# First product of six experts by Strassen's seven half-size products in a mixture-of-experts kernel

## The chip, the cores and the metric

One NeuronCore of a Trainium2 chip runs the whole program. The metric is device time in microseconds (us), the median of several executions of the same program; lower is better. TensorE is called PE here, its weight loads PEld, VectorE is DVE, ScalarE is ACT, GpSimd is POOL, SyncE is SP.

## The reference

Attention with a recurrent state gives one row of 320 numbers for each of 3072 tokens; a balanced gate gives each token a weight for each of 8 experts; every expert works on every token. The part that matters here is the experts:

```
N, D, E, F = (3072, 320, 8, 1024)
for e in range(E):
    h = np.maximum(x @ w1[e], 0.0)
    ye = h @ w2[e]
    out += P[:, e:e + 1] * ye
```

The gate `P` comes from 8 rounds of dividing by the row sums and then by the column sums ("P /= P.sum(1) + 1e-09", then "P /= P.sum(0) + 1e-09", then "P *= N / E").

## The kernel before

The attention runs first, in 24 units of 128 tokens, and expert 0 runs between its stages. Then come experts 1 to 7. The order of all work is a hand-written plan: `at(slot, fn)` puts a function into a numbered slot, and the slots are emitted in order of their number, so that every engine gets its instructions in this order and works through them strictly in turn. Engines wait for each other by semaphores.

Numbers in the experts are float32, multiplied as sums of a high and a low part (`w1h`, `w1l`, `hh`, `hl`). The activations x lie transposed in `xt`, 128 partitions by five rows of 3072 tokens: rows 0 and 1 are the high parts of the first 256 of the 320 dimensions, rows 2 and 3 their low parts, row 4 holds the high and the low part of the last 64 dimensions, one above the other.

A step of an expert is one block of 128 hidden units with 512 tokens (256 tokens in expert 0, and in the last two blocks of expert 7):

- `p1` (L103), the first product: 8 matmuls of 512 columns into one PSUM bank `ph`. Six are high*high, high*low and low*high for two halves of 128 dimensions; two are for the last 64 dimensions.
- `relu` (L112, L113): ACT makes `hh` from `ph`, then DVE makes `hl`.
- `p2` (L125), the second product: 12 matmuls of 320 columns (4 tiles of 128 tokens, 3 pairs of parts), with a slice of `hh` or `hl` as weights, summed over the 8 hidden blocks of the expert in four PSUM banks `py`.
- after the eighth hidden block `evac` (L137) adds `py` times the gate into `acc` on DVE, four tiles at a time.

`p1` runs two steps ahead of `p2`. Tokens are the outer loop, hidden blocks the inner one. The weights of the next expert are loaded by SP and split by POOL (L78 to L81) while an expert runs; expert 1's are split by ACT and POOL while expert 0 ends. The rounds of the gate (`sinkhorn`) stand in the plan at the change from expert 0 to expert 1, one stage each 1.25 slots: a stage `rows` is five DVE instructions on `logits` (L746 to L750), a stage `columns` is one small matmul pair on PE (`pc`, L753) and three DVE instructions (L755 to L757). The first such matmul follows `pb` (L740).

Of the kernel before, what the change touches and what calls it, by code (L numbers as in the profile page):

```python
# [16 lines left out]
def f32(ap):  # L17
    return ap.bitcast(F32)
# [3 lines left out]
def mlstm_moe_kernel(ctx, tc, q, k, v, i_gate, f_gate, o_gate, moe_w_gate, moe_w1, moe_w2, out):  # L22
# [16 lines left out]
    wa = ctx.enter_context(tc.tile_pool(name="wa", bufs=KF))  # L39
# [13 lines left out]
    wts = {}  # L53

    raws = {}

    def load_raw(pool, e, f):
        w1r = pool.tile([128, 3, 128], F32, tag="w1r", name="w1r")
        w2r = pool.tile([128, DM], F32, tag="w2r", name="w2r")
        cols = slice(f * 128, (f + 1) * 128)  # L60
        nc.sync.dma_start(w1r[:, 0:2, :], moe_w1[e, 0:256, cols].rearrange("(k p) f -> p k f", p=128))
        nc.sync.dma_start(w1r[0:DR, 2, :], moe_w1[e, 256:DM, cols])
        nc.sync.dma_start(w1r[DR:128, 2, :], moe_w1[e, 256:DM, cols])
        nc.sync.dma_start(w2r, moe_w2[e, cols, :])
        raws[e, f] = (w1r, w2r)

    def split_w(pool, e, f):
        """hi/lo parts of expert e's f-th 128 hidden columns."""
        w1r, w2r = raws.pop((e, f))
        w1h = pool.tile([128, 3, 128], F32R, tag="w1h", name="w1h")  # L70
        w1l = pool.tile([128, 3, 128], F32R, tag="w1l", name="w1l")
        w2h = pool.tile([128, DM], F32R, tag="w2h", name="w2h")
        w2l = pool.tile([128, DM], F32R, tag="w2l", name="w2l")
        if e == 1:
            nc.scalar.copy(w1h, w1r)
            nc.scalar.copy(w2h, w2r)
        else:
            nc.gpsimd.tensor_scalar(w1h, w1r, 1.0, 1.0, op0=ALU.mult, op1=ALU.mult)  # L78
            nc.gpsimd.tensor_scalar(w2h, w2r, 1.0, 1.0, op0=ALU.mult, op1=ALU.mult)
        nc.gpsimd.tensor_sub(w1l, w1r, f32(w1h))  # L80
        nc.gpsimd.tensor_sub(w2l, w2r, f32(w2h))  # L81
        wts[e, f] = (w1h, w1l, w2h, w2l)

# [1 line left out]
    class Moe:  # L85
        """Steps (expert, first tile, tiles, hidden blocks); the first product runs ahead of the second."""

        def __init__(self, hp, ps_h, ps_y):
            self.hp, self.ps_h, self.ps_y = hp, ps_h, ps_y
            self.h = {}  # L90
            self.y = {}

# [13 lines left out]
        def relu(self, e, t0, n, fs):  # L106
            nf = len(fs)
            ph = self.h[e, t0, fs]
            hh = self.hp.tile([128, nf, n * 128], F32R, tag="hh", name="hh")
            hl = self.hp.tile([128, nf, n * 128], F32R, tag="hl", name="hl")  # L110
            flat = lambda x: x.rearrange("p a t -> p (a t)")
            nc.scalar.activation(flat(hh), flat(ph), AF.Relu)  # L112
            nc.vector.scalar_tensor_tensor(flat(hl), flat(ph), 0.0, f32(flat(hh)), op0=ALU.max, op1=ALU.subtract)  # L113
            self.h[e, t0, fs] = (hh, hl)

        def p2(self, e, t0, n, fs):
            hh, hl = self.h.pop((e, t0, fs))
            if fs[0] == 0:
                self.y[e, t0] = [self.ps_y[j // 2].tile([128, 512], F32, tag="py", name="py") for j in range(n)]
            ys = self.y[e, t0]  # L120
            for a, f in enumerate(fs):
                _, _, w2h, w2l = wts[e, f]
                for w, h, first, last in ((w2h, hh, True, False), (w2l, hh, False, False), (w2h, hl, False, True)):
                    for j in range(n):
                        nc.tensor.matmul(ys[j][:, 0:DM], h[:, a, j * 128:(j + 1) * 128], w,  # L125
                                         start=f == 0 and first, stop=f == KF - 1 and last)
            if fs[-1] == KF - 1:
                self.evac(e, t0, n, self.y.pop((e, t0)))

        def evac(self, e, t0, n, ys):  # L130
            for j in range(n):
                t = t0 + j
                a, y = acc[:, t, :], ys[j][:, 0:DM]
                if e == 0:
                    nc.scalar.copy(a, y)
                    continue
                nc.vector.scalar_tensor_tensor(a, y, logits[:, t, e:e + 1], a, op0=ALU.mult, op1=ALU.add)  # L137
                if e == E - 1:
                    r = TILE_ROW[t]
                    nc.sync.dma_start(out[r * 128:(r + 1) * 128, :], a)  # L140

# [6 lines left out]
    def attention_phase():  # L148
        es = ExitStack()
        hp = ctx.enter_context(tc.tile_pool(name="hp", bufs=3))  # L150
# [9 lines left out]
        # (their scratch lies where the last tokens' sums come to lie)  # L160
# [26 lines left out]
        def gates_scan():  # L187
            """The running maximum, and the decay summed from each chunk's start."""
# [9 lines left out]
            # rows 0: the state's factor, 32: the key's factor in the next state, 64: the key's log weight  # L198
# [5 lines left out]
        def gates_rows():  # L204
            """The factors by token, and the states' over whole chunks."""
# [16 lines left out]
        def gate_weights():  # L222
            """The experts' gate weights: columns hi | lo."""
# [21 lines left out]
        def first_split(f, a):  # L245
            if a == 0:
                w1r = raw1[:, :, f * 128:(f + 1) * 128]
                w1h = wa.tile([128, 3, 128], F32R, tag="w1h", name="w1h")
                w1l = wa.tile([128, 3, 128], F32R, tag="w1l", name="w1l")
                nc.vector.tensor_copy(w1h, w1r)  # L250
                nc.gpsimd.tensor_sub(w1l, w1r, f32(w1h))
                wts[0, f] = (w1h, w1l) + wts[0, f]
            else:
                w2r = raw2[:, f, :]
                w2h = wa.tile([128, DM], F32R, tag="w2h", name="w2h")
                w2l = wa.tile([128, DM], F32R, tag="w2l", name="w2l")
                nc.vector.tensor_copy(w2h, w2r)
                nc.vector.tensor_sub(w2l, w2r, f32(w2h))
                wts[0, f] = (w2h, w2l)
# [32 lines left out]
        class Unit:  # L292
            """One chunk of one batch: its stages, each a method, in the order in which they run."""
# [23 lines left out]
            def split_hi(self, key):  # L317
                """First parts: q as (1, 2, 3) and (1, 1, 2), k as (3, 2, 1) and (2, 1, 1)."""
# [131 lines left out]
            def split_state(self, x):  # L450
                """The state's parts, as (3, 2, 1, 1)."""
# [53 lines left out]
        def gate(t0, n):  # L505
# [3 lines left out]
            # x's parts times both halves of the columns  # L509
# [281 lines left out]
```

## Time and profile before

| what | value |
|---|---|
| median of 3 runs | 1583.11 us (1582.42 to 1583.76) |
| span of the profiled execution, first to last instruction | 1580.5 us; its own device time is not listed, the median of the runs is 2.6 us above its span |
| PE busy | 1522.0 us, 96% of the span, 9719 matmuls |
| PEld busy | 1397.6 us, 88% |
| DVE busy | 633.3 us, 40% |
| ACT busy | 465.7 us, 29% |
| POOL busy | 378.7 us, 24% |
| mean granted clock of PE | 0.997 of full speed |

Busy time is the sum of the durations of an engine's instructions, and the share is of the span. A matmul row of the timeline gives the start of a group of like matmuls, the time from the first one's start to the last one's end, and their number; since matmuls are pipelined, the spacing of two starts is what one costs, and its duration is when its result is there. A bracket behind a row is the engine's idle time before it and what ended it.

### The profile page before, as it was taken

How to read it: one execution, taken by the hardware profiler on the slowest of the kernel's cores; microseconds unless marked ns; L12 is line 12 of the kernel's file. 1: busy time of each engine (PE TensorE's matmuls, PEld its weight loads, DVE VectorE, ACT ScalarE, POOL GpSimd, SP SyncE). 2: the span in 40 equal slices, each digit the busy share in tenths (PEclk: the TensorE clock that was granted, in tenths of full speed). 3: DMA queues.
4: the chain of work that ended last, by engine and by line, in shares of the span. 5: the costliest groups of instructions: out<-in, count | busy, mean ns of one | idle time of the engine just before them, and what ended most of it. 6: DMA issues, size and time to landing. Idle time of an engine off the chain costs nothing.

```text
span 1580.5 us, 24047 instructions
## 1 busy us (share of the span) xinstructions
PE 1522.0 (96%) x9719; PEld 1397.6 (88%) x9719; DVE 633.3 (40%) x1228; ACT 465.7 (29%) x976; POOL 378.7 (24%) x511
## 2 busy tenths in 40 slices
PE   3699999999999999999999999999999999999999
PEld 2699998998999999999999999999999999999998
DVE  5998898867222222222222222222222222222222
ACT  5677777733222211111111111111111111111111
POOL 5876676628100500031001400050003200000000
PEclk9999999999999999999999999999999999999999
DMA  9999999924000200011000200020001000000000
GB/s 207 210 193 197 198 176 186 190 56 130 27 1 1 74 1 1 0 44 30 1 0 8 67 1 1 1 70 5 0 1 34 13 1 1 1 0 17 34 18 34
DMA packets 271503, 88.12 MB, mean 56 GB/s; under 512 B 205440, under 2 KB 270784, under 8 KB 271392
## 3 DMA queue, kind: packets, MB, share of 16 engines
q1 hardware_dynamic: 271248, 86.29, 26.8%
q8 instruction: 76, 1.25, 0.3%
q10 hardware_dynamic: 144, 0.30, 0.1%
q14 instruction: 35, 0.29, 0.1%
HBM read 55.21 MB, written 6.18 MB: 39 GB/s over the span
## 4 chain that ended last, share of the span: by engine, by line
PE 84%; POOL 4%; DVE 4%; issue 3%; DMA 2%; ACT 2%; SPq 0%; DVEq 0%; POOLq 0%; ACTq 0%
PE ph L103 42%; PE py L125 39%; DMA kn<-in_k_dram 1%; DMA qs<-qp 1%; POOL pl L368 1%; POOL w L314 1%; PE pss L353 1%; POOL rk L327 1%; PE pyy L385 1%; POOL qn L327 0%; DVE den L480 0%; PE pyy L387 0%; DVE acc L484 0%; POOL qp L335 0%; POOL vv L375 0%
## 5 line engine op out<-in xcount | busy, mean ns | idle before, releaser
L113 DVE SCALAR_TENSOR_TENSOR hl<-ph,hh 128x512 fp32r<-128x512 f32 (+1 forms) x440 | 273.2, 621 | 890.1 <-ACT hh L112 889.9
L103 PE MATMUL ph<-xt,w1h 128*128 128x512 f32 (+1 forms) x2200 | 592.0, 366 | 0.9 <-DVE hl L113 0.9
L112 ACT ACTIVATE hh<-ph 128x512 fp32r<-128x512 f32 (+1 forms) x440 | 238.8, 543 | 1026.6 <-PE ph L103 1025.3
L103 PEld LDWEIGHTS ph<-xt,w1h 128*128 128x128 f32 x2200 | 380.0, 189 | 45.2 <-DVE hl L113 1.2
L103 PE MATMUL ph<-xt,w1l 128*128 128x512 f32 (+1 forms) x1320 | 403.5, 363 | 0.0
L125 PE MATMUL py<-w2h,hh 128*128 128x320 f32 x1536 | 300.6, 311 | 0.0
L125 PE MATMUL py<-w2h,hl 128*128 128x320 f32 x1536 | 296.8, 309 | 0.0
L125 PE MATMUL py<-w2l,hh 128*128 128x320 f32 x1536 | 296.8, 309 | 0.0
L103 PEld LDWEIGHTS ph<-xt,w1l 128*128 128x128 f32 x1320 | 241.8, 189 | 40.8
L125 PEld LDWEIGHTS py<-w2h,hh 128*128 128x128 f32 x1536 | 252.2, 189 | 26.6
L125 PEld LDWEIGHTS py<-w2l,hh 128*128 128x128 f32 x1536 | 243.6, 188 | 0.0
L125 PEld LDWEIGHTS py<-w2h,hl 128*128 128x128 f32 x1536 | 243.5, 188 | 0.0
L78 POOL TENSOR_SCALAR w1h<-w1r 128x384 fp32r<-128x384 f32 x48 | 24.9, 518 | 653.9 <-PE ph L103 653.9
L137 DVE SCALAR_TENSOR_TENSOR acc<-py,logits,acc 128x320 f32<-128x320 f32 x168 | 81.0, 544 | 2.1 <-PE py L125 2.1
L368 POOL TENSOR_TENSOR pl<-w,ph 128x512 fp32r<-128x512 f32 x48 | 63.1, 1314 | 57.2 <-ACT ph L367 57.1
L310 ACT ACTIVATE w<-w,gr 128x128 f32<-128x128 f32 x192 | 65.8, 393 | 1.5 <-DMA w<-gd 1.5
L80 POOL TENSOR_TENSOR w1l<-w1r,w1h 128x384 fp32r<-128x384 f32 x56 | 56.9, 1016 | 25.9 <-DMA w1r<-in_moe_w_dram 20.7
L353 PE MATMUL pss<-qs,ks 120*128 120x128 bf16 x384 | 33.2, 238 | 28.5 <-DMA ks<-kp 17.6
L387 PE MATMUL pyy<-vv,pl 128*128 128x42 f32 x192 | 53.2, 280 | 5.7 <-POOL pl L368 5.7
L385 PE MATMUL pyy<-vv,ph 128*128 128x84 f32 x192 | 54.1, 286 | 3.9 <-ACT ph L367 3.0
L353 PEld LDWEIGHTS <-ks 120*128 120x128 bf16 x384 | 25.3, 107 | 30.5 <-DMA ks<-kp 17.6
L81 POOL TENSOR_TENSOR w2l<-w2r,w2h 128x320 fp32r<-128x320 f32 x56 | 49.5, 884 | 0.0
(121 smaller groups left out, 930.2 us busy)
## 6 DMA issues: line engine op xcount, KB each, us to landing
w<-gd SPq DMA_DIRECT2D x24, 512.0 KB, 6.2
w2r<-in_moe_w_dram SPq DMA_DIRECT2D x56, 160.0 KB, 2.4
w1r<-in_moe_w_dram SPq DMA_DIRECT2D x56, 128.0 KB, 2.2
qn<-in_q_dram SPq DMA_DIRECT2D x24, 160.0 KB, 3.5
kn<-in_k_dram SPq DMA_DIRECT2D x24, 160.0 KB, 3.0
vn<-in_v_dram SPq DMA_DIRECT2D x24, 160.0 KB, 3.5
acc<-in_o_gate_dram SPq DMA_DIRECT2D x24, 160.0 KB, 3.2
out_dram<-acc SPq DMA_DIRECT2D x24, 160.0 KB, 1.8
```

The source lines that it names most:

```text
L80: nc.gpsimd.tensor_sub(w1l, w1r, f32(w1h))
L81: nc.gpsimd.tensor_sub(w2l, w2r, f32(w2h))
L103: nc.tensor.matmul(ph[:, a, :], w[:, kw, :], xt[:, kx, cols], start=i == 0, stop=i == len(seq) - 1)
L112: nc.scalar.activation(flat(hh), flat(ph), AF.Relu)
L113: nc.vector.scalar_tensor_tensor(flat(hl), flat(ph), 0.0, f32(flat(hh)), op0=ALU.max, op1=ALU.subtract)
L125: nc.tensor.matmul(ys[j][:, 0:DM], h[:, a, j * 128:(j + 1) * 128], w, start=f == 0 and first, stop=f == KF - 1 and last)
L137: nc.vector.scalar_tensor_tensor(a, y, logits[:, t, e:e + 1], a, op0=ALU.mult, op1=ALU.add)
L310: nc.scalar.activation(w[:, h, :], w[:, h, :], AF.Exp, bias=bias)
L353: nc.tensor.matmul(ps[:, j * L:(j + 1) * L], self.t["k"][0:3 * D, i, :], self.t["q"][0:3 * D, i, :], start=w == 0, stop=w == 1)
L368: nc.gpsimd.tensor_sub(flat(pl), p, f32(flat(ph)))
L385: nc.tensor.matmul(py[:, yo:yo + 2 * V2], ph[:, j, :], self.vv[:, h].rearrange("p a d -> p (a d)"), start=True, stop=False, skip_group_che ...
L387: nc.tensor.matmul(py[:, yo:yo + V2], pl[:, j, :], self.vv[:, h, 0, :], start=False, stop=True, skip_group_check=True)
```

## The change

Experts 2 to 7 take their first product in another way; the attention, expert 0's arithmetic and all second products keep theirs.

The unit of work is now (expert `e`, pair of hidden blocks `g`, pair of token blocks `p`): 256 hidden units and 1024 tokens, four of the old steps; there are 6*4*3 = 72. `g` is the outer loop, `p` the inner one. The first 256 dimensions, the 256 hidden units and the 1024 tokens are cut in half each, and the eight half-size products become seven by Strassen's scheme (Winograd's form). Each product is 3 matmuls of 512 columns (`product`), the last 64 dimensions are added by 4*2 matmuls (`rest`). Four PSUM banks A, B, C, D take the products, DVE adds them up with the sums `u2`, `u3`, `c22` in SBUF (L259), and ACT, DVE and POOL make the four pairs `hh`, `hl` (L266 to L271). The two halves of the second product are 24 matmuls each (`second`): half 0 at the end of the unit, half 1 in the middle of the next unit. Its banks are summed into `acc` after each pair of hidden blocks, 8 tiles a unit, not after eight blocks.

The sums of x that Strassen needs are made once (`combine`, POOL and ACT, while expert 1 runs), those of the weights once for each (e, g) (`w_sums` on POOL, `w_split` on ACT and POOL, 24 times). Expert 1 goes through all tokens twice, with hidden blocks 0 to 3 and then 4 to 7; weights and `hh`, `hl` share one tile `wz`; and the stages of the gate stand (x1 + 10.9 - o) / 19 = 0.93 slots apart, where they were 1.25 apart.

The core of the diff (allocation, loads and placing of weights are left out):

```diff
+        def w_sums(self, e, g):
+            st = late["st"].rearrange("p (a f) -> p a f", f=128)
+            for o, x, y in ((T1, W12, W11), (T3, W22, W12), (WRD, WR1, WR2), (T2, W22, T1), (T4, W21, T2)):
+                nc.gpsimd.tensor_sub(st[:, o, :], st[:, x, :], st[:, y, :])
...
+            nc.scalar.copy(w[:, 0:n], r)
+            nc.gpsimd.tensor_sub(w[:, n:2 * n], r, f32(w[:, 0:n]))
...
+            for i, (s, m) in enumerate(((0, hi), (0, lo), (1, hi))):
+                nc.tensor.matmul(ps, w1[:, s, w - 1, :], m, start=start and i == 0, stop=i == 2, skip_group_check=True)
...
+            for s in range(2):
+                nc.tensor.matmul(ps, w1[:, s, w - 1, :], xt[:, 4, col], start=False, stop=s == 1, skip_group_check=True)
...
+            for a in blocks:
+                h = self.HS[half * 2 + a]()
+                hh, hl = h[:, 0:512], h[:, 512:1024]
+                seq += [(w2[:, 0, a, :], hh), (w2[:, 1, a, :], hh), (w2[:, 0, a, :], hl)]
+            order = [(i, j) for i in range(6) for j in range(4)]
+            if tiles_outer:
+                order = [(i, j) for j in range(4) for i in range(6)]
+            for i, j in order:
+                w, h = seq[i]
...
+            mul = lambda slot, n, x, w, start=True: do(slot, lambda: self.product(bank(n), e, g, p, x, w, start))
+            rem = lambda slot, n, half, w: do(slot, lambda: self.rest(d[n], e, g, p, half, w))
+            add = lambda slot, o, x, n: do(slot, lambda: nc.vector.tensor_add(tp(o), d[n], tp(x)))
+            def h_parts(slot, half, a, n=None, x=None, clamp=False):
+                h = self.HS[half * 2 + a]()
+                hh, hl = h[:, 0:512], h[:, 512:1024]
+                src = lambda: d[n] if n else tp(x)
+                if clamp:
+                    do(slot, lambda: nc.scalar.activation(tp(x), tp(x), AF.Relu))
+                    do(slot, lambda: nc.scalar.copy(hh, tp(x)))
+                    do(slot, lambda: nc.gpsimd.tensor_sub(hl, tp(x), f32(hh)))
+                else:
+                    do(slot, lambda: nc.scalar.activation(hh, src(), AF.Relu))
+                    do(slot + 0.05, lambda: nc.vector.scalar_tensor_tensor(hl, src(), 0.0, f32(hh), op0=ALU.max, op1=ALU.subtract))
+            mul(0, A, (0, 0), W11)
+            do(0.5, lambda: nc.scalar.copy(tp(u2), d[A]))
+            mul(1, B, S2, T2)
+            add(1.5, u2, u2, B)
+            mul(2, C, S3, T3)
+            rem(2, C, 1, WR2)
+            add(2.5, u3, u2, C)
+            mul(3, D, S1, T1)
+            add(3.5, c22, u3, D)
+            mul(5, D, S4, W22, False)
+            rem(5, D, 0, WR2)
+            add(5.5, u2, u2, D)
+            h_parts(5.6, 0, 1, x=u2)
+            mul(6, C, (1, 1), T4)
+            rem(6, C, 1, WRD)
+            add(6.5, u3, u3, C)
+            mul(7, A, (1, 0), W21, False)
+            rem(7, A, 0, WR1)
+            h_parts(7.5, 0, 0, n=A)
+            h_parts(7.7, 1, 1, x=c22, clamp=True)
+            h_parts(7.8, 1, 0, x=u3, clamp=True)
+            def half(i):
+                ys = [self.ps_y[j // 2].tile([128, 512], F32, tag="py", name="py") for j in range(4)]
+                self.second(e, g, p, i, ys, (1, 0), i == 1)
+                for j in range(4):
+                    evac(e, (2 * p + i) * 4 + j, ys[j], e == E - 1 and g == NG - 1)
+            do(8, lambda: half(0))
+            return out_, lambda: half(1)
...
+        whole(t[0], 0, 1)
+        whole(t[1], 1, 1)
+        nc.gpsimd.tensor_add(t[2], t[0], t[1])
+        whole(t[3], 0, 0)
+        nc.gpsimd.tensor_sub(t[4], t[3], t[0])
+        nc.gpsimd.tensor_sub(t[5], t[2], t[3])
+        split(S1, t[2])
+        whole(t[0], 1, 0)
+        split(S3, t[4])
+        nc.gpsimd.tensor_sub(t[1], t[0], t[5])
+        split(S2, t[5])
+        split(S4, t[1])
...
-        for fn in sinkhorn(late):
+        stages = sinkhorn(late)
+        step = (x1 + 10.9 - o) / len(stages)
+        for fn in stages:
             at(o, fn)
-            o += LATE["sinkhorn_step"]
+            o += step
...
+        def prep(x, e, g):
+            at(x, fast.w_load, e, g)
+            at(x + 3.1, fast.w_sums, e, g)
+            at(x + 4.1, fast.w_split, e, g, 0)
+            at(x + 4.2, fast.w_split, e, g, 1)
+        todo = [(e, g) for e in range(2, E) for g in range(NG)]
+        prep(x - 12, *todo[0])
+        for i, (e, g) in enumerate(todo):
+            for p in range(3):
+                if p == 1 and i + 1 < len(todo):
+                    prep(x + 0.9, *todo[i + 1])
+                items, rest = fast.unit(e, g, p)
+                for slot, fn in items:
+                    at(x + slot, fn)
+                at(x + 4, tail.pop())
+                tail.append(rest)
+                x += 9
```

What order the engines get shows at three places. First PE inside the experts, before: the rows of one step (`ph` is the first product, `py` the second).

```order
L103 MATMUL ph<-xt,w1h 128x512 x4
L103 MATMUL ph<-xt,w1l 128x512 x2
L103 MATMUL ph<-xt,w1h 128x512
L103 MATMUL ph<-xt,w1l 128x512
L125 MATMUL py<-w2h,hh 128x320 x4
L125 MATMUL py<-w2l,hh 128x320 x4
L125 MATMUL py<-w2h,hl 128x320 x4
```

PE inside the experts, now: one unit from its first product on (psA to psD are the banks; L218 is `product`, L224 is `rest`; the `py` row in the middle is half 1 of the unit before).

```order
L218 MATMUL psA<-xt,wz 128x512 x3
L218 MATMUL psB<-xs,wz 128x512 x3
L218 MATMUL psC<-xs,wz 128x512 x3
L224 MATMUL psC<-xt,wz 128x512 x2
L218 MATMUL psD<-xs,wz 128x512 x3
L239 MATMUL py<-wz 128x320 x24
L218 MATMUL psD<-xs,wz 128x512 x3
L224 MATMUL psD<-xt,wz 128x512 x2
L218 MATMUL psC<-xt,wz 128x512 x3
L224 MATMUL psC<-xt,wz 128x512 x2
L218 MATMUL psA<-xt,wz 128x512 x3
L224 MATMUL psA<-xt,wz 128x512 x2
```

The row after these is half 0, 24 more `py` matmuls, and then the next unit's psA. Where four steps had 32 matmuls of 512 columns and 48 of 320, a unit has 29 and 48.

Second DVE in the same unit, now (before, it had eight `hl` of L113 and then four sums of L137 for each block of 512 tokens):

```order
L259 TENSOR_TENSOR tp<-psB,tp 128x512
L259 TENSOR_TENSOR tp<-psC,tp 128x512
L259 TENSOR_TENSOR tp<-psD,tp 128x512
L158 SCALAR_TENSOR_TENSOR acc<-py,logits,acc 128x320 x4
L259 TENSOR_TENSOR tp<-psD,tp 128x512
L271 SCALAR_TENSOR_TENSOR wz<-tp,wz 128x512
L259 TENSOR_TENSOR tp<-psC,tp 128x512
L271 SCALAR_TENSOR_TENSOR wz<-psA,wz 128x512
L158 SCALAR_TENSOR_TENSOR acc<-py,logits,acc 128x320 x4
```

`tp` holds u2, u3 and c22, and `wz` here the pairs `hh`, `hl`. Five additions of a bank are new, and a tile is summed into `acc` four times for each expert instead of once.

Third PE at the change from expert 0 to expert 1, between matmuls of the gate (`pc`), before:

```order
L753 MATMUL pc<-cs,onesf 128x8
L125 MATMUL py<-w2h,hh 128x320 x2
L125 MATMUL py<-w2l,hh 128x320 x2
L125 MATMUL py<-w2h,hl 128x320 x2
L103 MATMUL ph<-xt,w1h 128x512 x4
L103 MATMUL ph<-xt,w1l 128x512 x2
L103 MATMUL ph<-xt,w1h 128x512
L103 MATMUL ph<-xt,w1l 128x512
L125 MATMUL py<-w2h,hh 128x320 x2
L125 MATMUL py<-w2l,hh 128x320 x2
L125 MATMUL py<-w2h,hl 128x320 x2
L753 MATMUL pc<-cs,onesf 128x8
```

And now, at the same steps of expert 1:

```order
L964 MATMUL pc<-cs,onesf 128x8
L146 MATMUL py<-wz,h_72 128x320 x6
L116 MATMUL ph<-xt,xs 128x512 x8
L964 MATMUL pc<-cs,onesf 128x8
L146 MATMUL py<-xs,wz 128x320 x12
L116 MATMUL ph<-xt,xs 128x512 x8
L964 MATMUL pc<-cs,onesf 128x8
```

One first and one second product lie between two `pc` now, where three products lay between them at this place before. All eight `pc` now come before the sixth step of expert 1; before, three of them came after it.

## Rows read from the trace of the kernel before

**Rows 1.** The page, part 1: busy time, share of the span, instructions

```profile
PE 1522.0 (96%) x9719; PEld 1397.6 (88%) x9719; DVE 633.3 (40%) x1228; ACT 465.7 (29%) x976; POOL 378.7 (24%) x511
```

**Rows 2.** The page, part 4: the chain that ended last, by engine

```profile
PE 84%; POOL 4%; DVE 4%; issue 3%; DMA 2%; ACT 2%; SPq 0%; DVEq 0%; POOLq 0%; ACTq 0%
```

**Rows 3.** Windows: stretch; PE, PEld, DVE, ACT, POOL busy; clock; DMA

```profile
150.00:200.00 50.00, 46.84 (x434) 45.36 (x434) 41.58 (x97) 37.36 (x94) 34.18 (x47) 0.97 1.05 190
...
700.00:800.00 100.00, 100.00 (x559) 90.72 (x558) 25.13 (x40) 16.77 (x28) 15.29 (x22) 1.00 0.09 24
1000.00:1100.00 100.00, 100.00 (x558) 90.59 (x557) 26.99 (x44) 16.24 (x28) 22.01 (x32) 1.00 0.10 30
```

**Rows 4.** Timeline of one step: start, us, engine, line, count, [idle]

```profile
1000.88 1.09 PE L103 MATMUL ph<-xt,w1h 128*128 128x512 f32 x4
...
1002.49 0.39 PE L103 MATMUL ph<-xt,w1l 128*128 128x512 f32 x1
...
1002.71 0.74 PE L125 MATMUL py<-w2h,hh 128*128 128x320 f32 x4
1002.91 0.60 ACT L112 ACTIVATE hh<-ph 128x512 fp32r<-128x512 f32 x1 [2.99 <-PE ph L103]
...
1003.54 0.69 DVE L113 SCALAR_TENSOR_TENSOR hl<-ph,hh 128x512 fp32r<-128x512 f32 x1 [2.90 <-ACT hh L112]
...
1004.47 0.39 PE L103 MATMUL ph<-xt,w1h 128*128 128x512 f32 x1
```

**Rows 5.** Groups by form: busy us, mean ns, idle before

```profile
L137 DVE SCALAR_TENSOR_TENSOR acc<-py,logits,acc 128x320 f32<-128x320 f32 x168 | 81.0, 544 | 2.1 <-PE py L125 2.1
...
L368 POOL TENSOR_TENSOR pl<-w,ph 128x512 fp32r<-128x512 f32 x48 | 63.1, 1314 | 57.2 <-ACT ph L367 57.1
...
L81 POOL TENSOR_TENSOR w2l<-w2r,w2h 128x320 fp32r<-128x320 f32 x56 | 49.5, 884 | 0.0
...
L359 DVE TENSOR_TENSOR w<-pss,w 128x512 f32<-128x512 f32 x48 | 32.5, 677 | 2.0 <-POOL w L314 1.9
...
L534 ACT ACTIVATE acc<-acc 128x1280 f32<-128x1280 f32 x5 | 6.4, 1274 | 0.1
...
L534 ACT ACTIVATE acc<-acc 128x640 f32<-128x640 f32 x2 | 1.5, 736 | 0.0
```

**Rows 6.** Timeline of PE, 150 to 200 us

```profile
190.20 0.64 PE L103 MATMUL ph<-xt,w1h 128*128 128x256 f32 x4
...
191.15 0.46 PE L125 MATMUL py<-w2h,hh 128*128 128x320 f32 x2
...
195.12 0.61 PE L353 MATMUL pss<-qs,ks 120*128 120x128 bf16 x8 [2.12 <-DVE xt L501]
```

**Rows 7.** One line's durations: ns min/median/max, first and last start

```profile
L749 DVE TENSOR_TENSOR logits<-logits,rs x8: 358/643/1210, 361.2 to 392.1; 128x192 f32<-128x192 f32 x8
```

**Rows 8.** Timeline of PE at the gate's rounds, 358 to 402 us

```profile
358.93 0.38 PE L740 MATMUL pb<-m,onesf 1*128 1x1 f32 x2
...
362.20 0.39 PE L753 MATMUL pc<-cs,onesf 128*128 128x8 f32 x2
...
363.40 1.09 PE L103 MATMUL ph<-xt,w1h 128*128 128x512 f32 x4
...
366.02 0.39 PE L753 MATMUL pc<-cs,onesf 128*128 128x8 f32 x2 [0.62 <-DVE cs L750]
...
370.17 0.39 PE L753 MATMUL pc<-cs,onesf 128*128 128x8 f32 x2
...
374.09 0.28 PE L753 MATMUL pc<-cs,onesf 128*128 128x8 f32 x2
...
381.73 1.09 PE L103 MATMUL ph<-xt,w1h 128*128 128x512 f32 x4
...
400.79 1.09 PE L103 MATMUL ph<-xt,w1h 128*128 128x512 f32 x4
```

**Rows 9.** Windows of PE: stretch; PE busy; granted clock; DMA

```profile
193.00:194.00 1.00, 0.00 (x1) 1.00 1.28 290
...
197.00:198.00 1.00, 1.00 (x9) 0.50 1.06 303
```

More of the change, by code (lines that the diff above doesn't have):

```diff
@@ L67, in split_w @@
[L67 to L76, printed above, removed]
[L77 to L79 removed]
+    W1S, W2S = 2 * 768, 2 * DM
@@ L117, in p2 @@
             hh, hl = self.h.pop((e, t0, fs))
-            if fs[0] == 0:
+            (f,) = fs
+            first, last = (f == 0, f == KF - 1) if e == 0 else (f % 4 == 0, f % 4 == 3)
+            if first:
                 self.y[e, t0] = [self.ps_y[j // 2].tile([128, 512], F32, tag="py", name="py") for j in range(n)]
             ys = self.y[e, t0]
[L121 to L140, printed above, removed]
+            _, _, w2h, w2l = wts[e, f]
@@ new lines, in p2 @@
+            seq = [(w2h, hh), (w2l, hh), (w2h, hl)]
+            order = [(i, j) for i in range(3) for j in range(n)]
+            if last and e:
+                order = [(i, j) for j in range(n) for i in range(3)]
+            for i, j in order:
+                w, h = seq[i]
+                nc.tensor.matmul(ys[j][:, 0:DM], h[:, 0, j * 128:(j + 1) * 128], w,
+                                 start=first and i == 0, stop=last and i == 2)
+            if last:
+                ys = self.y.pop((e, t0))
+                for j in range(n):
+                    evac(e, t0 + j, ys[j], False)
@@ new lines, in combine, with whole, split @@
+    def combine(p, q):
+        S1, S2, S3, S4 = range(4)
+        tp = late["tp"].rearrange("p a t -> p (a t)")
+        t = [tp[:, a * 256:(a + 1) * 256] for a in range(6)]
+        col = [slice((2 * p + half) * 512 + q * 256, (2 * p + half) * 512 + (q + 1) * 256) for half in range(2)]
+        to = slice(q * 256, (q + 1) * 256)
+        xs = late["xs"]
+        def whole(o, k, half):
+            nc.gpsimd.tensor_add(o, f32(xt[:, k, col[half]]), f32(xt[:, k + 2, col[half]]))
+        def split(i, x):
+            hi, lo = xs[:, p, i, 0, to], xs[:, p, i, 1, to]
+            nc.scalar.copy(hi, x)
+            nc.gpsimd.tensor_sub(lo, x, f32(hi))
+        whole(t[0], 0, 1)
[10 more added lines that the diff above has]
+        split(S4, t[1])
@@ L694, in attention_phase @@
[L694 to L703 removed]
+            at(max(o, x1 + 2 + 8 * (t // 4) + 2 * (t % 4)), weigh_first, t)
@@ L704, in attention_phase @@
+        for a in range(2):
+            at(x1 + 16 + 14 * a, combine, 0, a)
+            at(x1 + 54 + 11 * a, combine, 1, a)
+            at(x1 + 76 + 10 * a, combine, 2, a)
+        x = x0
+        tail = []
         for i in range(len(steps) + look):
```

183 lines of the change are left out of this document (131 added, 52 removed).

## The prediction

> **What bounds the kernel now.** I read the page from the whole to the part. Part 1 gives PE 96% of the span and 9719 matmuls [rows 1]; the reader should take from it only that PE is the candidate, since a busy share is an average. Part 4, the chain of waits, puts 84% of the span on PE [rows 2]. The windows settle it: in 700 to 800 us and in 1000 to 1100 us PE is busy for 100.00 of 100 us at the full clock, with DVE at 25 to 27, ACT at 16 to 17 and POOL at 15 to 22 [rows 3]. So in experts 1 to 7 nothing is waited for; a matmul less is time less, and work on the other three engines is free until it makes PE wait. The timeline of one step prices PE: from 1000.88 to 1002.71 the 8 matmuls of the first product, 0.229 us each, and from 1002.71 to 1004.47 the 12 of the second, 0.147 us each; a step is 3.59 us [rows 4].
>
> **The saving.** A unit does what four steps did, with 29 matmuls of 512 columns in place of 32, and the same 48 of 320. Three matmuls less are 3 * 0.229 = 0.69 us, and 72 units give 49.4 us, if no unit makes PE wait. A unit is then 29 * 0.229 + 48 * 0.147 = 13.68 us.
>
> **Does a unit make PE wait?** I lay one unit out from the start of A, in PE's new order, with the durations of the rows: A 0 to 0.69, B to 1.37, C to 2.52, D to 3.20, half 1 of the unit before to 6.72, D again to 7.87, C to 9.01, A to 10.15, half 0 to 13.68. A result is there 0.39 us after the start of its last matmul [rows 4]. ACT on 512 elements takes 0.60, DVE's pair instruction 0.69 [rows 4]; an addition of a bank and SBUF on DVE is like L359, 0.68; a sum into `acc` is 0.54; POOL's subtraction of 512 is 1.31 [rows 5].
> - Half 0 starts with the pair made from u2. D's result is there at 8.03, the addition ends at 8.74 and the relu at 9.37; needed at 10.15, so 0.78 to spare. Its low part ends on DVE at about 10.1, needed after eight matmuls, at 11.33: 1.2 to spare.
> - The pair from A: result 10.31, relu to 10.94, needed after twelve matmuls of half 0, at 11.91: about 1.0 to spare.
> - Half 1 needs c22 and u3 through ACT (two instructions each, the last ends at 13.35) and POOL (ends at 14.8); it starts in the next unit, at 16.88: 2 to spare.
> - Banks: half 0's four sums run from the last matmuls on to 1.6 of the next unit, and half 1 wants those banks at 3.20; D is read by 4.08 and filled again from 6.72.
>
> So PE waits nowhere, and the least margin is 0.78 us. The queues hold: DVE has 5 * 0.68 + 2 * 0.69 + 8 * 0.54 = 9.1 us of 13.68, where it had 25 to 27% of 14.36 us, 3.6 to 3.9 [rows 3]; ACT 7 * 0.60 = 4.2; POOL 2.6. In one unit of three the weights of the next pair come on top. From L81 and L368, (1314 - 884) / 192 = 2.24 ns per element and 167 ns fixed [rows 5], I estimate for POOL five subtractions of 128 elements at 0.45 us, one of 1280 at 3.03 and one of 640 at 1.60, in all 6.9 us; ACT's two copies are like L534, 1.27 and 0.74 us [rows 5]. POOL is through with the unit before at 1.1, makes the sums until about 3.4, and ACT, idle since 1.48, copies until 5.4, before it is wanted for u2 at 8.74. These loads are issued by SP, which has nothing else queued until the output of the last pair, as soon as the last split has freed the buffer, two units ahead. I put all of it at nothing; the cover is PE's own 13.68 us, and if it were gone each tenth of a microsecond a unit would cost 7.2 us. That DVE and ACT at a high load slow the matmuls themselves has no support: with DVE at 41.6, ACT at 37.4 and POOL at 34.2 of 50 us [rows 3], 8 matmuls of 256 columns went from 190.20 to 191.15, 0.119 us each, about half of the 512 [rows 6].
>
> **DVE against POOL.** One line of the trace speaks against the change: L749, which reads two operands from SBUF, took between 0.358 and 1.210 us for the same shape [rows 7], while POOL was splitting weights. The excess, 0.85 us, is about one L81 (0.88). In the unit only the pair from u2 has two SBUF operands on DVE, at 9.4 to 10.1, and in one unit of three POOL's last long subtraction ends at about 9.4 to 9.6. A delay of 0.2 us falls within the 1.2 us to spare, so the sum takes nothing; a delay d costs d - 1.2 in each of 23 units. [...]
>
> **Experts 0 and 1.** The plan's order up to the gate is the same on every engine. Expert 1's second pass adds 24 sums into `acc` on DVE, 13 us beside 172 us of PE. `combine` holds ACT for about 3.7 us six times (four copies that wait for four POOL subtractions, 0.74 us each by the same estimate); a bank of the first product is wanted 5.35 us after it is full, relu and hl take 1.3, so ACT may be 4 us late. Nothing. The smaller tiles that ended expert 7 vanish (about 0.7 us less), but now half 1 of the last unit follows half 0 directly and waits about 0.5 us for its low part. Nothing in sum.
>
> **The gate's rounds get closer.** This is the cost that I do count. The profile shows how fast a round can go: from `pc` to `pc` it took 3.82, 4.15 and 3.92 us at 362.20, 366.02, 370.17 and 374.09, and PE waited for DVE before the second (0.62) [rows 8]; the chain of eight DVE instructions and one hl is the bound there. Now only a second product (0.88, later 1.76 us) and a first product (0.95, later 1.83) lie between two `pc`: about 1.8 us, then 2.7 three times, 3.6 twice and 1.8 (no `p1` between the last two). PE must wait in nearly all of them. The first `pc` follows `pb` by the chain of 358.93 to 362.20, as before. Seven rounds of 3.96 us (the mean) put the last `pc` at 389.9, and the sixth first product of expert 1 starts behind it at 390.1. Before it started at 381.73: 8.4 us later. The three `pc` that came after it then cost 19.06 us for five steps (381.73 to 400.79) where five steps are 17.95: 1.1 us, which goes [rows 8]. Net +7.3, I take +7. Bounds: rounds of 3.5 us give +4, of 4.4 us +10.
>
> **PE's clock there.** [...] The new waits are about 2 us and less. I add 1 us for one such fall, partly hidden in the waits, from 0 (none) to 3 (two).
>
> **The sum.** -49.4 + 7 + 1 = -41.4 us. It is made against the profiled execution with its span of 1580.5; the median of the runs, 1583.11, is 2.6 us above that span, so the new median would be 1541.7, a span of about 1539.
>
> **Rivals.**
> 1. The gate's rounds cost nothing (0.1): if its DVE instructions run near 0.36 us now that POOL has half as much to split there, and PE's wait is absorbed. Then 1583.1 - 49.4 = 1533.7. Against it: the 0.62 us wait with three products per round.
> 2. POOL blocks DVE's pair from u2 (0.13). If the splits are 1 to 3 us later than laid out, the subtraction of 1280 stands in the way: with d = 2 the loss is 0.8 * 23 = 18 us, 1560; with the full 3.03 it is 42 us, 1584. For it: rows 7. Against it: POOL's queue leaves the splits early.
> 3. Slower: the hand-over before half 0 (0.08). Matmul result, DVE addition, ACT relu stand in a row before half 0 of all 72 units, with 0.78 us to spare. It decides at 0.78 + 0.57 = 1.35 us more than laid out: from there 72 waits eat the remaining 41.4 us. With a wait of 1 us, 1541.7 + 72 = 1614. For it: three engines in a row, and half 1's sums stand before the addition in DVE's queue. Against it: each link has its row, and those sums end 0.65 us earlier.
>
> That the seven products are not fewer matmuls is excluded by the order of PE's instructions.
>
> **How the numbers follow.** Forecast as summed, 0.65; the rivals 0.10, 0.13 and 0.08; the rest, 0.04, is unnamed. The range holds the forecast with its bounds (1537 to 1548), the first rival and rival 2 up to d = 2: 1531 to 1560. About 3.2 us (0.2%) is what a measurement can tell from no change. Faster: 0.65 + 0.10 + most of rival 2 and of the rest = 0.90; same 0.02; slower 0.08.
>
> **What would show it.** Right: in the experts' windows PE at 100 of 100 us, A to A 13.7 us, DVE near 65%; `pc` to `pc` near 3.9 us with idle time of PE before most. Wrong: idle time of PE before L239 released by ACT or DVE (rival 3), an L271 from `tp` of over 1.5 us (rival 2), or matmuls of 512 columns further apart than 0.229 us.

## The result, and the profile after

| | before | after |
|---|---|---|
| median | 1583.05 us (1582.42 to 1583.76) | 1539.64 us (1537.95 to 1543.2) |
| ratio to before, 95% interval | | 0.9727 (0.9713 to 0.9741) |
| profiled execution | span 1580.5 us | 1538.51 us, span 1536.7 |
| unit of 256 hidden units by 1024 tokens | 14.37 us (four steps) | 13.65 us |

The kernel is 43.4 us faster; 1541.7 was forecast, inside a range of 1531 to 1560.

Page of the changed kernel, part 1 and the first line of part 4, as [rows 1, 2]:

```profile
PE 1474.2 (96%) x9439; PEld 1357.8 (88%) x9439; DVE 1007.0 (66%) x1892; ACT 640.4 (42%) x1256; POOL 640.0 (42%) x703
...
PE 84%; DVE 4%; POOL 4%; DMA 3%; issue 2%; ACT 1%; SPq 1%; POOLq 0%; ACTq 0%; DVEq 0%
```

The shares of PE are the same 96% and 84% as before and would not tell the two kernels apart. The windows do. Changed kernel; stretch, its length, then busy us of PE, PEld, DVE, ACT, POOL, granted clock, DMA share, GB/s:

```profile
360.00:380.00 20.00, 15.51 (x81) 12.71 (x80) 15.74 (x45) 6.45 (x15) 11.22 (x14) 0.91 0.29 82
380.00:400.00 20.00, 18.55 (x103) 16.22 (x103) 12.56 (x35) 5.55 (x11) 0.00 (x0) 1.00 0.00 1
700.00:800.00 100.00, 100.00 (x568) 91.49 (x567) 64.74 (x111) 32.57 (x53) 31.14 (x28) 1.00 0.05 16
1000.00:1100.00 100.00, 100.00 (x568) 91.57 (x568) 64.91 (x111) 34.46 (x55) 36.34 (x35) 1.00 0.05 15
```

Against [rows 3]: in the experts PE is still busy for all of 100 us, while DVE went from 25 to 27 up to 65 and POOL from 15 to 22 up to 31 to 36. Between the attention and the last unit it is only at the gate (360 to 400 us) that PE stands idle, for 5.9 us, and there the granted clock falls (0.91 over 20 us).

One unit in the timeline of the changed kernel (start, us, engine, line, count, idle before), from the last D to half 0 and on to the next A:

```profile
1003.35 0.86 PE L218 MATMUL psD<-xs,wz 128*128 128x512 f32 x3
...
1004.05 0.62 PE L224 MATMUL psD<-xt,wz 128*128 128x512 f32 x2
...
1004.71 0.69 DVE L259 TENSOR_TENSOR tp<-psD,tp 128x512 f32<-128x512 f32 x1 [0.61 <-PE psD L224]
...
1005.43 0.63 ACT L270 ACTIVATE wz<-tp 128x512 fp32r<-128x512 f32 x1 [7.32 <-DVE tp L259]
...
1006.55 3.64 PEld L239 LDWEIGHTS py<-wz 128*128 128x128 f32 x24
...
1006.78 3.68 PE L239 MATMUL py<-wz 128*128 128x320 f32 x24
...
1010.29 0.86 PE L218 MATMUL psA<-xt,wz 128*128 128x512 f32 x3
```

ACT's relu of u2 ends at 1006.06 and half 0 starts at 1006.78, so 0.72 us lie between them (0.78 was laid out). One row up stands what my layout had left out: the first weights of half 0, which are that relu's result, are loaded from 1006.55 on, 0.23 us before the matmul. The experiments show how much was really to spare.

**Where the 43.8 us between the two spans came from.** I cut every profiled execution at the same two marks of PE's timeline: `pb`, a small matmul pair that opens the gate's rounds, and the sixth full first product of expert 1 (381.73 us before [rows 8], 390.84 after). The stretches here and in the experiments are differences of these starts and of the span, in us.

| kernel | start to `pb` | `pb` to sixth product | from there to the end |
|---|---|---|---|
| before | 358.93 | 22.80 | 1198.8 |
| after | 360.08 | 30.76 | 1145.9 |
| difference | +1.2 | +8.0 | -52.9 |

### The profile page after: what moved, and what is told of

Same layout as the page of the kernel before. It is cut to its first block, busy times and chain, and to the rows that moved or that the text cites. A ratio compares the mean times of both kernels' runs of the same rounds, so it can differ in the third digit from the quotient of the medians.

```text
span 1536.7 us, 24718 instructions
## 1 busy us (share of the span) xinstructions
PE 1474.2 (96%) x9439; PEld 1357.8 (88%) x9439; DVE 1007.0 (66%) x1892; ACT 640.4 (42%) x1256; POOL 640.0 (42%) x703
## 4 chain that ended last, share of the span: by engine, by line
PE 84%; DVE 4%; POOL 4%; DMA 3%; issue 2%; ACT 1%; SPq 1%; POOLq 0%; ACTq 0%; DVEq 0%
PE py L239 33%; PE ph L116 8%; PE py L146 8%; PE psD L218 6%; PE psA L218 6%; PE psC L218 6%; PE psC L224 4%; PE psB L218 3%; PE psD L224 2%; PE psA L224 2%; DMA qs<-qp 2%; DMA kn<-in_k_dram 1%; POOL pl L557 1%; PE pss L542 1%; POOL w L503 1%
## 5 line engine op out<-in xcount | busy, mean ns | idle before, releaser
L158 DVE SCALAR_TENSOR_TENSOR acc<-py,logits,acc 128x320 f32<-128x320 f32 x624 | 320.2, 547 | 197.8 <-PE py L239 196.8
L268 POOL TENSOR_TENSOR wz<-tp,wz 128x512 fp32r<-128x512 f32 x144 | 183.8, 1297 | 620.3 <-ACT wz L267 620.3
L239 PE MATMUL py<-wz 128*128 128x320 f32 x1728 | 264.9, 309 | 0.3 <-DVE acc L158 0.3
L239 PE MATMUL py<-h,wz 128*128 128x320 f32 x1728 | 264.8, 309 | 0.0
L239 PEld LDWEIGHTS py<-wz 128*128 128x128 f32 x1728 | 259.0, 188 | 6.0 <-issue 0.5
L239 PEld LDWEIGHTS py<-h,wz 128*128 128x128 f32 x1728 | 259.0, 188 | 5.6
L116 PE MATMUL ph<-xt,wz 128*128 128x256 f32 (+1 forms) x960 | 160.7, 311 | 0.9 <-DVE h L128 0.9
L116 PEld LDWEIGHTS ph<-xt,wz 128*128 128x128 f32 x960 | 138.0, 194 | 7.5 <-DVE h L128 1.1
L259 DVE TENSOR_TENSOR tp<-psD,tp 128x512 f32<-128x512 f32 x144 | 99.6, 692 | 51.2 <-PE psD L224 43.4
L218 PE MATMUL psD<-xs,wz 128*128 128x512 f32 x432 | 122.3, 391 | 0.0
L218 PE MATMUL psA<-xt,wz 128*128 128x512 f32 x432 | 122.3, 391 | 0.0
L259 DVE TENSOR_TENSOR tp<-psC,tp 128x512 f32<-128x512 f32 x144 | 99.0, 687 | 30.8 <-PE psC L224 30.2
L266 ACT ACTIVATE tp<-tp 128x512 f32<-128x512 f32 x144 | 90.2, 626 | 0.0
L224 PE MATMUL psC<-xt,wz 128*128 128x512 f32 x288 | 88.7, 389 | 0.0
L218 PEld LDWEIGHTS psA<-xt,wz 128*128 128x128 f32 x432 | 78.2, 188 | 11.4
L218 PEld LDWEIGHTS psD<-xs,wz 128*128 128x128 f32 x432 | 78.2, 188 | 11.4
```

The lines of the kernel that those rows point to most:

```text
L116: nc.tensor.matmul(ph[:, a, :], w[:, kw, :], xt[:, kx, cols], start=i == 0, stop=i == len(seq) - 1)
L218: nc.tensor.matmul(ps, w1[:, s, w - 1, :], m, start=start and i == 0, stop=i == 2, skip_group_check=True)
L224: nc.tensor.matmul(ps, w1[:, s, w - 1, :], xt[:, 4, col], start=False, stop=s == 1, skip_group_check=True)
L239: nc.tensor.matmul(ys[j][:, 0:DM], h[:, j * 128:(j + 1) * 128], w, start=i == 0, stop=i == 5)
L259: add = lambda slot, o, x, n: do(slot, lambda: nc.vector.tensor_add(tp(o), d[n], tp(x)))
L266: do(slot, lambda: nc.scalar.activation(tp(x), tp(x), AF.Relu))
```

## Experiments on the unit

**Take the saving back.** One of the seven products is done twice, so that a unit has 32 matmuls of 512 columns again.

```diff
             mul(1, B, S2, T2)
+            mul(1.1, B, S2, T2)
```

> The changed kernel, but the product into bank B is computed twice in each unit, so that a unit has again 32 matmuls of 512 columns. If PE alone sets the pace in experts 2 to 7 and the gain is three matmuls a unit, the three come back in full: 72 * 3 * 0.229 = 49 us more than the changed kernel, 1589 us. If the units had slack on PE (PE waiting for banks or operands), part of the 49 us would disappear in it, and the time would stay below 1575.

Measured: 1588.53 us (1586.05 to 1590.57), ratio to before 1.0032 (1.0021 to 1.0044). The stretch from the sixth product to the end is 1194.8 us against 1145.9: 48.9 us, 0.680 a unit, 0.227 a matmul. Three matmuls a unit are the saving, and nothing else in the units pays it back. From A to A a unit takes 14.33 us here, 0.04 less than four steps with the same matmuls. With as many of these matmuls as before, the kernel is 5.5 us slower than before: the price of the gate's place, less what else the change gained.

**Eat the margin before half 0.** ACT's relu of u2 is done twice, and in a second run three times, which makes the hand-over longer by 0.63 and by 1.26 us.

```diff
-                    do(slot, lambda: nc.scalar.activation(hh, src(), AF.Relu))
+                    for _ in range(1 if n else 2):
+                        do(slot, lambda: nc.scalar.activation(hh, src(), AF.Relu))
```

> The changed kernel, with the ACT instruction that makes hh from u2 done twice in every unit (0.63 us more between DVE's addition and half 0). The trace of the changed kernel shows 0.72 us from the end of this instruction to the start of half 0. If that is real slack, no change: 1540 us within 3. If the hand-over was already the bound, 72 * 0.6 = 45 us more, 1585.

> As the last, with that instruction done three times (1.26 us more). The slack of 0.72 us is used up and PE should wait some 0.55 us at half 0 of each unit: 72 * 0.55 = 40 us more than the changed kernel, 1580, idle time of PE before L239 released by ACT. If PE's queue has other slack, it stays at 1540.

Measured: twice, 1547.81 us (1547.04 to 1549.88), 8 us more than the changed kernel where the same was expected; three times, 1595.14 us (1592.9 to 1597.87), 55 us more where 40 were expected, ratio to before 1.0079 (1.0059 to 1.0099). By the last stretch of the table the two lost 9.1 and 55.7 us, 0.126 and 0.774 us in each of 72 units. So 0.632 - 0.126 = 0.51 and 1.264 - 0.774 = 0.49 us were to spare, not 0.72: the margin ends at the weight load. The kernel with two relus, the idle time at L239 by what ended it (us, times), and then its timeline:

```profile
  ACT wz L271: 19.3, 72
```

```profile
1010.50 3.52 PEld L239 LDWEIGHTS py<-wz 128*128 128x128 f32 x24 [0.27 <-ACT wz L271]
1010.50 3.79 PE L239 MATMUL py<-wz 128*128 128x320 f32 x24
```

The wait is at the weight load, in every unit, and the row of the matmuls shows none: it starts with the load and is only 0.11 us longer. The windows of that kernel say PE 100.00 of 100 us from 1000 to 1100. With three relus the matmuls' own row shows a part of it too:

```profile
1002.92 3.52 PEld L239 LDWEIGHTS py<-h,wz 128*128 128x128 f32 x24 [0.93 <-ACT wz L271]
1002.93 3.79 PE L239 MATMUL py<-h,wz 128*128 128x320 f32 x24 [0.51 <-ACT wz L271]
```

So rival 3's mechanism exists, and the kernel is 0.5 us away from it, not 0.78. It turns the gain into a loss at 0.5 + 0.6 = 1.1 us more; with 1.26 us more it did.

**Put POOL's long subtraction in DVE's way.** The subtraction of 1280 elements is done twice, which moves POOL's work some 3 us back.

```diff
-            nc.gpsimd.tensor_sub(w[:, n:2 * n], r, f32(w[:, 0:n]))
+            for _ in range(1 if x else 2):
+                nc.gpsimd.tensor_sub(w[:, n:2 * n], r, f32(w[:, 0:n]))
```

> The changed kernel, with POOL's subtraction of 1280 elements done twice in a row (2.97 us more on POOL in one unit of three), so that POOL is still subtracting when DVE wants its only instruction with two SBUF operands (the pair from u2). If DVE and POOL exclude each other, that instruction (0.69 us so far) waits for the end of the running subtraction, about 1.2 us, or for two of them, about 2.8 us: its longest time would be 1.9 to 3.5 us, and PE would lose between 0 and 1.7 us in each of 23 units, 1540 to 1579 us. If they don't, it stays at 0.69 us and the time at 1540.

Measured: 1543.83 us (1542.47 to 1544.77), 4 us more. DVE's pair from u2 in the changed kernel and in this one (ns min/median/max, first and last start), first the changed kernel:

```profile
L271 DVE SCALAR_TENSOR_TENSOR wz<-tp,wz x72: 691/692/695, 555.6 to 1524.9; 128x512 fp32r<-128x512 f32 x72
```

```profile
L272 DVE SCALAR_TENSOR_TENSOR wz<-tp,wz x72: 691/695/2115, 557.8 to 1531.0; 128x512 fp32r<-128x512 f32 x72
```

And one collision in the timeline of the kernel with the doubled subtraction:

```profile
607.77 6.01 POOL L203 TENSOR_TENSOR wz<-st,wz 128x1280 fp32r<-128x1280 f32 x2 [1.38 <-ACT wz L201]
...
612.47 1.85 DVE L272 SCALAR_TENSOR_TENSOR wz<-tp,wz 128x512 fp32r<-128x512 f32 x1 [0.70 <-ACT wz L271]
...
613.73 2.02 POOL L203 TENSOR_TENSOR h<-st,h 128x640 fp32r<-128x640 f32 x1
614.38 2.35 PEld L240 LDWEIGHTS py<-wz 128*128 128x128 f32 x16 [0.16 <-DVE wz L272]
```

DVE's instruction starts while POOL is at work and ends at 614.32, 0.5 us after POOL's subtraction: it takes 1.85 us, 0.69 when undisturbed. POOL's next one, 1.57 us when undisturbed, takes 2.02. Beside the same two subtractions of POOL, DVE's sum at 609.92 and its addition at 611.08, which read a bank of PSUM, kept their 0.55 and 0.69 us. In the changed kernel the two miss each other narrowly: POOL's last split of a unit with weights ends at 1019.53 and the pair starts at 1019.75.

The price goes the same way as at the relu. From start of relu to start of relu a unit takes 13.65 us; most of the 23 units with a collision take 13.79 to 13.83 at a delay of 1.14 to 1.16 (1.83 to 1.85, less 0.69), and one took 14.08 at 1.42. So 1.0 us was to spare for the low part, where I had laid out 1.2: again about 0.2 us less, as at half 0, where the weight load comes 0.23 us ahead of the matmul. Over the last stretch that is 3.9 us.

## Experiments on the gate's rounds

PE's timeline of the changed kernel at the gate, as [rows 8]; `pc` is the product of a round, L116 with 8 matmuls the first product of expert 1:

```profile
360.08 0.38 PE L951 MATMUL pb<-m,onesf 1*128 1x1 f32 x2
...
363.42 0.39 PE L964 MATMUL pc<-cs,onesf 128*128 128x8 f32 x2 [1.82 <-DVE cs L961]
...
367.33 0.39 PE L964 MATMUL pc<-cs,onesf 128*128 128x8 f32 x2 [1.59 <-DVE cs L961]
...
368.54 3.46 PE L116 MATMUL ph<-xt,xs 128*128 128x512 f32 x8
...
390.60 0.39 PE L964 MATMUL pc<-cs,onesf 128*128 128x8 f32 x2 [1.36 <-DVE cs L961]
...
390.84 2.10 PE L116 MATMUL ph<-xt,xs 128*128 128x512 f32 x8
```

From the first `pc` to the eighth are 27.18 us, 3.88 us a round (3.96 forecast), with PE waiting for DVE before five of them, and one product at half the clock (3.46 us, with a granted clock of 0.50 from 369 to 370 us). Before, one round waited, 0.62 us.

**Only the spacing, in the kernel before.** The rounds are put as close as in the changed kernel; everything else stays.

```diff
-            prep0=2, prep1=2.75, prep_step=2.25, sinkhorn=2.75, sinkhorn_step=1.25)
+            prep0=2, prep1=2.75, prep_step=2.25, sinkhorn=2.75, sinkhorn_step=0.93)
```

> The kernel before, with one edit alone: the stages of the gate 0.93 slots apart as in the changed kernel, not 1.25. If the closer rounds are a cost of their own, PE waits at them: 7 to 8 us slower than before, about 1590.5 us, with about 3.9 us from pc to pc. If they are hidden, no change, 1583.

Measured: 1594.06 us (1592.61 to 1599.31), ratio to before 1.0072 (1.005 to 1.0095): 11 us more, where 7 to 8 were expected. `pb` to the sixth product went from 22.80 to 33.42. The closeness of the rounds, in a kernel that is otherwise the old one, costs 10.6 us there; the changed kernel lost 8. A round took 4.26 us here instead of 3.88; POOL is busy for 30.2 of the 40 us from 360 to 400 in this kernel, and for 11.2 in the changed one, which would be a reason, but no run separates it.

**Fewer rounds.** Four of the eight are left out.

```diff
-        return [top, top_row, top_all] + [rows, columns] * 8
+        return [top, top_row, top_all] + [rows, columns] * 4
```

> The changed kernel with four rounds of the gate in place of eight, spread over the same slots (four rounds are left out). The stages stand 1.6 slots apart, so that PE has a third product or more between two pc. If the closeness of the rounds costs about 7.6 us, most of this comes back, and four pairs of small matmuls (about 1 us) go: 1531 to 1534 us. If it costs nothing, 1539.

Measured: 1532.8 us (1532.51 to 1533.43), ratio to before 0.9672 (0.9649 to 0.9695). `pb` to the sixth product is 22.90 us, what it was before the change, and the rest 1145.8. The loss of 8 us goes with the close rounds; nothing else in this stretch has a part in it that shows.

**Shorter rounds.** The two additions of 1e-9 in a round are left out, two DVE instructions of eight.

```diff
-            nc.vector.tensor_scalar_add(rs, rs, 1e-9)
...
-            nc.vector.tensor_scalar_add(rc, tl["pc"][:, 0:E], 1e-9)
-            nc.vector.reciprocal(rc, rc)
+            nc.vector.reciprocal(rc, tl["pc"][:, 0:E])
```

> The changed kernel without the two additions of 1e-9 in a round of the gate (two of DVE's eight instructions; both are below the last digit of the sums in float32). If DVE's chain sets the pace of the rounds, a round gets shorter by about 0.5 us, from about 3.9 to 3.4, and PE waits some 4 us less over the rounds, perhaps without the fall of its clock: 1534 to 1537 us. If PE's waits there have another cause, 1540.

Measured: 1538.53 us (1537.45 to 1541.18), ratio to before 0.9711 (0.969 to 0.9733), an interval that overlaps the changed kernel's. By stretches the rounds did get shorter: 28.32 us instead of 30.76, a gain of 2.4 where 4 were expected. In this profiled execution the attention took 3.0 us longer up to `pb` (363.05), which hides it in the span. And the first rounds did not get as short as laid out, 3.66 and 3.76 us from `pc` to `pc` where 3.4 were expected; DVE's timeline of this kernel:

```profile
364.87 0.93 DVE L959 TENSOR_TENSOR logits<-logits,rs 128x192 f32<-128x192 f32 x1
...
367.05 1.08 DVE L966 SCALAR_TENSOR_TENSOR logits<-logits,rc 128x192 f32<-128x192 f32 x1
...
370.72 1.00 DVE L966 SCALAR_TENSOR_TENSOR logits<-logits,rc 128x192 f32<-128x192 f32 x1
...
374.48 0.36 DVE L966 SCALAR_TENSOR_TENSOR logits<-logits,rc 128x192 f32<-128x192 f32 x1
```

Up to 371.72 us three instructions that take 0.36 later take about 1, as L749 in [rows 7]; POOL is busy for 12.1 of the 20 us from 360 to 380, and for none of the next 20.

**Wide spacing in the changed kernel.** The rounds are spread out again, to 4.96 us from `pc` to `pc` (365.19 to 399.91 us; 4.45 before the change). Four sums of expert 1 would then come before their gate is there; ACT copies them aside and DVE adds them later with their weight. The weighing of expert 0's sums moves to other slots with them.

```diff
-                    evac(e, t0 + j, ys[j], False)
+                    if e == 1 and t0 == 0 and f < 4:
+                        nc.scalar.copy(stash(j), ys[j][:, 0:DM])
+                    else:
+                        evac(e, t0 + j, ys[j], False)
...
-        step = (x1 + 10.9 - o) / len(stages)
+        step = (x1 + 18.9 - o) / len(stages)
...
+                at(x1 + 21.3 + 2 * t, unstash, t)
```

> The changed kernel with its gate rounds spread out again to about 4.4 us apart (step from x1+18.9 instead of x1+10.9); expert 1's first finished block of tokens is therefore copied aside unweighted and added with its weight later, four ACT copies and four DVE additions more. Theory: the 8 us that the changed kernel lost between the gate's first product and the sixth step of expert 1's first product (30.76 us against 22.80 before) are TensorE's waits for DVE's rounds, 5.8 us, and one step at half clock, 1.46 us; with the old spacing this stretch goes back to 23 to 25 us and the kernel takes 1531 to 1535 us. Rival: the loss belongs to the crowding of POOL, which splits weights beside the rounds until about 375 us whatever their spacing; then the first three rounds stay late, the stretch takes 28 us or more, and the time is 1537 to 1540.

> The same, with the two additions of 1e-9 in each round left out. Theory: with room between the rounds their length no longer matters, so it differs from the wider spacing alone by no more than 2 us: 1530 to 1535. Rival (crowding): each round is shorter by about 0.5 us, and the time is 2 to 4 us below that of the wider spacing alone.

> The changed kernel as it is, beside the two, for a comparison on one chip: 1538 to 1542.

| kernel (one chip, before 1582.91 us) | median | ratio to before | `pb` | to sixth product | to the end |
|---|---|---|---|---|---|
| changed kernel again | 1539.26 (1537.78 to 1540.02) | 0.9719 (0.9705 to 0.9732) | 359.86 | 30.99 | 1145.9 |
| wide spacing | 1534.12 (1532.97 to 1536.62) | 0.9689 (0.9676 to 0.9703) | 359.68 | 25.31 | 1146.1 |
| wide spacing, no additions | 1531.02 (1529.63 to 1532.43) | 0.9665 (0.9652 to 0.9678) | 361.60 | 23.22 | 1145.9 |

PE's waits for the rounds in the kernel with the wide spacing (us in total, times, longest), then its first rounds in PE's timeline:

```profile
PE pc L981 <- DVE cs L978: 2.1, 1, 2.1
```

```profile
365.19 0.39 PE L981 MATMUL pc<-cs,onesf 128*128 128x8 f32 x2 [2.15 <-DVE cs L978]
366.55 3.42 PE L116 MATMUL ph<-xt,xs 128*128 128x512 f32 x8
370.69 0.28 PE L981 MATMUL pc<-cs,onesf 128*128 128x8 f32 x2
```

Five waits became one (six in the changed kernel's second profile). 5.7 us of the lost 8 came back, and the kernel takes 5.1 us less than the changed one, with the whole computation done; it beats both. The rival, that POOL's splits alone make the rounds late, falls: they are there as before, until 368 us, and cost nothing once the rounds have room. The step without additions missed its bound of 2 us: 3.1 us less, inside the 2 to 4 that had been set for the rival of crowded rounds. The table puts 2.1 of it before the sixth product, and there the rounds are not crowded: seven of the eight wait for nothing in either kernel, the first still waits (1.62 us instead of 2.15), and no product ran at half the clock, where the kernel with additions lost 1.4 us on one (366.55, 3.42 us instead of 2.00; granted clock 0.50 from 367 to 369 us). The last 1.0 us stays open. Room makes the length of seven rounds free, not that of the first, whose chain starts at `pb`.

## Why the prediction was right, and where it was off

**The bound** was right. The experts stay at 100 of 100 us on PE with DVE at 65, as laid out, and a product added takes 0.680 us a unit.

**The saving** of -49.4 was too small a term: a unit measures 13.65 us and four steps 14.37, so 72 units give -51.8. The product done twice costs 0.680 us a unit, so three matmuls are 49.0 us, about as priced. The other 2.8 us, 0.04 us a unit, I had not seen. They lie where PE changes between products of 512 and of 320 columns, four times in a unit and eight times in four steps. PE's timeline of the changed kernel from B on (its A starts at 1010.29, above):

```profile
1010.99 0.85 PE L218 MATMUL psB<-xs,wz 128*128 128x512 f32 x3
1011.68 0.84 PE L218 MATMUL psC<-xs,wz 128*128 128x512 f32 x3
...
1013.49 3.68 PE L239 MATMUL py<-wz 128*128 128x320 f32 x24
```

The six matmuls of A and B stand 0.232 us apart, the eight after them 0.226. From 700 to 1500 us it is the same in both kernels: behind a change to 512 columns the first five spacings are 0.231, 0.236, 0.228, 0.232 and 0.231 us and all later ones 0.227, so 0.025 us more in sum; behind a change to 320 columns the first four are 0.005 us less in sum. Two such pairs fewer in a unit are the 0.04 us, and the kernel with the product done twice shows them too, with 14.33 for 14.37 us. Why the first spacings are longer stays open.

That ends the last stretch at -52.9: -51.8, about 0.4 of the five steps that follow the sixth product (18.69 us instead of 19.06 us; 1.1 was forecast), and the rest at the tail. What is missing at the five steps is a wait that the change brought: expert 1's first sums into `acc` now come after four hidden blocks, and there a second product waits for banks:

```profile
396.38 2.54 PE L146 MATMUL py<-xs,wz 128*128 128x320 f32 x12
...
396.87 0.19 PEld L146 LDWEIGHTS py<-xs,wz 128*128 128x128 f32 x1 [0.27 <-DVE acc L158]
397.32 1.33 PEld L146 LDWEIGHTS py<-xs,wz 128*128 128x128 f32 x9 [0.27 <-DVE acc L158]
...
398.75 2.00 PE L116 MATMUL ph<-xt,xs 128*128 128x512 f32 x8
```

Its twelve matmuls take 2.37 us instead of 1.76, 0.6 us more. In the kernel before with close rounds, which has no such sums there, the five steps took 18.05 us: 1.0 of the 1.1 went, as laid out.

**The margin** of 0.78 us before half 0 and of 1.2 us for the low part stand at 0.5 and 1.0 us. The forecast rests on neither being used up, and holds; but I counted to the matmul's start, and what waits is its weight load, some 0.2 us earlier. Rival 3's point of decision is 1.1 us, not 1.35.

**DVE against POOL** was right in its place: the pair never took over 0.695 us, and at 1019 us POOL's last split ends 0.2 us before it. The delay that [rows 7] let me expect is real: moved into POOL's way, the pair took up to 2.115 us, and a delay d cost d - 1.0 in the units it met (d - 1.2 was laid out), with d up to 1.42. A delay of 3.03 us, the far end of rival 2, no run shows.

**The gate's rounds**: +7 forecast, +7.6 measured (8.0 up to the sixth product, less 0.4 behind it), with 3.88 us a round for 3.96. In the six profiles that have this gate unedited the stretch took 30.76 to 31.66 us, so the 8.0 is the least of them. Rival 1 fell, and the wide spacing shows why: with room for the rounds the time is close to its 1533.7 (1534.12). That the two agree to 0.4 us is chance: 2.5 us were still lost at the gate there, and the units saved 2.4 more than either sum had.

**PE's clock**: one fall, as forecast, but its +1 us was an estimate, and no run shows it as a cost of its own: the fall was nearly all hidden in the waits. In the changed kernel's first profile the granted clock was 0.50, as in [rows 9], the fall cost 1.46 us (3.46 instead of 2.00) and the waits came to 5.8 us; its second profile has no such fall, waits of 7.4 us, and about the same length of the stretch, 30.99 against 30.76. The rounds set the pace there, so a slower PE mostly waits less. Four other kernels with this gate (product done twice, subtraction done twice, relu done twice and three times) ran slower for longer: a second product of six matmuls took 1.95 us in each of them, where it took 1.12 in the changed kernel, and with two relus the granted clock was 0.50 for 6 us in a row. Their stretch took 31.23, 31.45, 31.66 and 31.48 us: at most 0.7 us more than without a fall. PE's window of the kernel with two relus (busy, clock, DMA share, GB/s):

```profile
362.00:368.00 6.00, 5.40 (x21) 0.50 0.56 151
```

**Nothing for the start** was off by 1.2 us; the attention's length differs by more than that from profile to profile (last section), so nothing shows that the change is the cause. The sum of the stretches, +1.2 + 8.0 - 52.9, is -43.8 (rounded); -41.4 was forecast. The saving's 2.4 us are the difference; the start's +1.2 and the 1.1 us less at the gate and the tail nearly cancel.

## What to carry to other kernels

Where an engine is busy for all of its time, price an algorithm that saves instructions by their spacing (0.227 us a matmul here, where its duration is 0.39), and then look at what the new order pushes together elsewhere: here 8 us of the saving were paid where the gate had to be done sooner, and 5 of them came back by letting its first users wait aside. Count the slack of a hand-over to PE up to the weight load, not the matmul (0.23 us earlier here), and read the idle time of PEld: with two relus, PE at 100 of 100 us hid 0.13 us a unit. Cut a trace at marks that every variant has; the stretches told apart differences that the total time could not.

## What the runs showed of the hardware that I had not expected

- A wait for weights need not show at the matmuls: with two relus, PEld waited 0.27 us in each of 72 units, 19.3 us in all, and the time rose by 8 us without idle time on PE from 1000 to 1100 us. In the changed kernel the load of half 0 starts at 1006.55, 0.23 us ahead of its own matmul and while A's last matmuls (1006.32 to 1006.93) are in flight.
- The attention's length changes from one profiled execution to the next by more than several of the effects here: `pb` came between 358.11 and 363.05 us in twelve profiles. Its cause stayed open. A spread of this size can also hide a difference of 2.4 us in one stretch from the medians.
- The clock at the gate: after waits of 1.82 and 1.59 us the product from 368.54 on ran at a granted clock of 0.50; the second profile of the same kernel had waits of 2.02 and 1.40 us at the same places and stayed at 1.00. PE's windows of the first profile (busy, clock, DMA share, GB/s):

```profile
367.00:368.00 1.00, 0.67 (x5) 1.00 0.27 67
...
369.00:370.00 1.00, 1.00 (x4) 0.50 0.49 145
```

and of the second:

```profile
367.00:368.00 1.00, 0.88 (x6) 1.00 0.43 125
...
369.00:370.00 1.00, 1.00 (x6) 1.00 0.58 167
```
